# A gated pair of linear-attention blocks on one core: x's first blocks in two transfers, and the gate's weights ahead of x

## Chip, core and metric

The kernel runs on one core of a Trainium2 chip. The metric is the time of one execution in microseconds of device time; the number that counts is the median of several executions. Beside it stands the profile of one execution of its own, taken by the hardware profiler.

## What is computed

x has 2048 rows of 640 columns in bfloat16. Two attention blocks, A and B, read the same x, each with its own wqkv (640 x 1920) and wo (640 x 640). In a block there are 32 heads of 20 columns, and the attention is linear: no softmax, but a positive function phi on q and k. A gate, one number for each row of x, mixes the two outputs.

```
g = sigmoid((x * gate_w).sum(-1, keepdims=True))
a = block(x, A_wqkv, A_wo);  b = block(x, B_wqkv, B_wo)
return g * a + (1 - g) * b

block(x, wqkv, wo):
    q, k, v = heads of x @ wqkv
    pq, pk = phi(q), phi(k)              # phi(t) = (t + 1 if t > 0 else exp(t)) + 1e-6
    kv = sum over rows of pk * v;  z = sum over rows of pk
    o = (pq @ kv) / (pq . z + 1e-6)
    return o @ wo
```

## The kernel before

x lies in SBUF twice: xn has rows on the partitions, xT has columns on the partitions (five groups c of 128). k of A is computed in 16 blocks of 128 rows: for each block and each half (320 columns) five matmuls, one for each c, with xT's block as weights and wkA's part c as the moving operand (`k_mm`, line 288). Then come q, the sums over rows, and block B in the same way; the last stage forms the output rows. The order of the work is written out by hand (line 942 on), so each engine works its instructions off in the order of the program.

**The loads at the start** (lines 151 to 174). `load_x(eng, lo, hi)` loads blocks lo to hi of x's first 512 rows into xn. These rows are dealt out so that a partition holds four rows that follow each other in memory, one for each block; one block is 160 KB in pieces of 1280 bytes. `load_wk(eng, lo, hi)` loads wkA's parts lo to hi, 160 KB each. Two queues issue, SyncE (SP) and ScalarE (ACT), in this order:

- SP: block 0 of x, wkA part 0, the gate's weights g5 (1.2 KB, five partitions), wkA part 2, wkA parts 3 and 4 in one, three transfers of wqA, then 15 transposing loads (line 172) that bring the other 1536 rows of x straight into xT.
- ScalarE: block 1 of x, wkA part 1, blocks 2 and 3 of x, then the load of its table of functions.

**The first work on PE.** Seven matmuls on constants (line 206) fill the time until x arrives. `k_first` (line 311) then transposes x's blocks on PE: `x_transpose` (line 242) is five transpositions of 128 x 128 into PSUM and two copies by VectorE into xT. `gate_column` (line 217) is one more transposition, of g5, from which three small ScalarE copies (line 222) put the gate's weights beside wkA as a further column, so that the second half of each k block carries the gate's product along (321 columns). The order in `k_first` is: blocks 0 and 1 transposed, the gate column, k for blocks 0 and 1 with parts 0 and 1 of wkA (8 matmuls), block 2 transposed, part 2 for blocks 0 and 1 (4 matmuls), block 3 transposed, parts 0 to 2 for block 2 (6 matmuls), and then parts 3 and 4 for blocks 0, 1 and 2, each followed by phi on ScalarE and VectorE (`k_done`, line 295). A whole block 3 and q follow.

**Much later**, `Masks` (line 1015) runs the matmuls that are the last to read wvA and then loads wvB through `load_w` (line 859), whose last argument says where the load is cut. wvB is first read in `kv_low` (line 1056).

Of the kernel before, what the change touches and what calls it, by code (L numbers as in the profile page):

```python
# [9 lines left out]
P = 128  # L10
# [7 lines left out]
DT = D // P  # L18
ST = S // P
NB = 4  # L20
CB = 4
# [12 lines left out]
def kernel(  # L34
# [11 lines left out]
    nc = tc.nc  # L46
# [29 lines left out]
    def ps_raw(name, slot=None):  # L76

        if slot is None:
            slot = turn[0]
            turn[0] = (slot + 1) % 4  # L80
        return pools.get(slot, pools["ps"]).tile([P, 4 * HB], BF16, tag=f"ps{slot}", name=name)
# [5 lines left out]
    def ps(name, slot=None):  # L87

        return banks(ps_raw(name, slot))
# [20 lines left out]
    g5 = persist.tile([DT, P], BF16, name="g5")  # L110
# [37 lines left out]
    wv = [None, None]  # L148
    wq = [None, None]
    wk[0] = wpool.tile([P, DT, D + 2], BF16, tag="wk", name="wkA")  # L150
    def load_x(eng, lo, hi):
        eng.dma_start(out=xn[:, lo:hi, :], in_=xb0[:, lo:hi, :])

    def load_wk(eng, lo, hi):
        eng.dma_start(out=wk[0][:, lo:hi, 0:D], in_=wq_dram[0][:, lo:hi, D:2 * D])

    load_x(nc.sync, 0, 1)
    load_x(nc.scalar, 1, 2)
    load_wk(nc.sync, 0, 1)
    load_wk(nc.scalar, 1, 2)  # L160
    nc.sync.dma_start(out=g5[:], in_=gate_w.rearrange("(c p) -> c p", p=P))
    load_x(nc.scalar, 2, 3)
    load_wk(nc.sync, 2, 3)
    load_x(nc.scalar, 3, 4)
    nc.scalar.preload_act_table_set("natural_log_exp_and_others")
    load_wk(nc.sync, 3, DT)
    wq[0] = wpool.tile([P, DT, D], BF16, tag="wq", name="wqA")
# [2 lines left out]
    for n in range(1, NB):  # L170
        for c in range(DT):
            nc.sync.dma_start_transpose(
                out=xT[:, c, n * HB:(n + 1) * HB], in_=x2[n * HB:(n + 1) * HB, c * P:(c + 1) * P]
# [4 lines left out]
    for r in range(4):  # L178
# [3 lines left out]
        out=spread[:].rearrange("p (h t) -> p h t", t=TW), in_=I4[:, :, None].to_broadcast([P, H, TW])  # L182
    )
    nc.gpsimd.memset(maskE[:], 1.0)
    for lo in range(0, HF, K6):
        part = maskE[:, lo:min(lo + K6, HF)]
        for sign, base in ((1, 0), (-1, Dh - 1)):
            nc.gpsimd.affine_select(
                out=part, in_=part, pattern=[[-sign * Dh, part.shape[1] // Dh], [0, Dh]],
# [3 lines left out]
    for rows, n in ((slice(0, 2 * H), H // 2), (slice(2 * H, P), H)):  # L193
        nc.gpsimd.tensor_copy(
            out=E4_rows[rows, 0:n], in_=I4[rows, 0:n, None].to_broadcast([rows.stop - rows.start, n, Dh])
# [6 lines left out]
    warm_raw = ps_raw("warm", 0)  # L202
# [14 lines left out]
    def gate_column(pt):  # L217

        at = slice(4 * HB - 2 * P, 4 * HB - 2 * P + DT)
        nc.tensor.transpose(out=pt[:, at], in_=g5[:], identity=ident[0:DT, 0:DT])  # L220
        for lo, hi in ((0, 1), (1, 2), (2, DT)):
            nc.scalar.copy(out=wk[0][:, lo:hi, D:D + 1], in_=pt[:, at, None][:, lo:hi])
# [19 lines left out]
    def x_transpose(i, slot):  # L242
        pt = ps_raw("xt", slot)
        for c in range(DT):
            nc.tensor.transpose(out=pt[:, c * P:(c + 1) * P], in_=xn[:, i, c * P:(c + 1) * P], identity=ident[:])
        src = pt[:, 0:D].rearrange("p (c n) -> p c n", c=DT)
        for lo, hi in ((0, 2), (2, DT)):
            nc.vector.tensor_copy(out=xT[:, lo:hi, i * P:(i + 1) * P], in_=src[:, lo:hi])

    class Phi:  # L250

        def __init__(self, dst, src, lifted=False):
            self.dst, self.src, self.lifted = dst, src, lifted
            e = work.tile([P] + list(dst.shape[1:]), BF16, tag="e", name="e", bufs=4)
            self.e = e[:]
            self.parts = parts = [(self.e, dst, src)] if not isinstance(src, list) else [
                (self.e[:, n], dst[:, n], part) for n, part in enumerate(src)]
            for to, lifted_to, part in parts:
                nc.scalar.activation(out=to, in_=part, func=ACT.Exp)  # L259
                if lifted is True:  # L260
                    self.lift(lifted_to, part)
# [26 lines left out]
    def k_mm(b, i, c, pt, hf):  # L288
        n = HF + (b == 0 and hf == 1)
        nc.tensor.matmul(  # L290
            pt[:, hf, 0:n], lhsT=xT[:, c, i * P:(i + 1) * P], rhs=wk[b][:, c, hf * HF:hf * HF + n],
            start=(c == 0), stop=(c == DT - 1),
        )

    def k_done(b, i, pt, lifted=False, between=None):
        f = Phi(pk[:, i, :].rearrange("p (b n) -> p b n", b=2), pt[:, :, 0:HF], lifted)
        if b == 0:
            nc.scalar.activation(out=gl[:, i:i + 1], in_=pt[:, 1, HF:HF + 1], func=ACT.Exp)
        f.clamp()
        if between is not None:  # L300
            between()
        f.top()

    def k_chunk(b, i, slot=None, lifted=False, between=None):
        pt = ps(f"k{'AB'[b]}", slot)
        for hf in range(2):
            for c in range(DT):
                k_mm(b, i, c, pt, hf)
        k_done(b, i, pt, lifted, between)

    def k_first():

        pts = []

        def part(i, cs, hfs=(0, 1)):
            for c in cs:
                for hf in hfs:
                    k_mm(0, i, c, pts[i], hf)

        x_transpose(0, 3)  # L320
        x_transpose(1, 1)
        gate_column(warm_raw)
        pts += [ps("kA", 2), ps("kA", 3)]
        for hf in range(2):
            for i in range(2):
                part(i, (0, 1), (hf,))
        x_transpose(2, 0)
        for i in range(2):
            part(i, (2,))
        x_transpose(3, 1)  # L330
        pts.append(ps("kA", 0))
        part(2, (0, 1, 2))
        for i in range(3):
            part(i, (3, 4))
            k_done(0, i, pts[i])
        k_chunk(0, 3, 1)
# [281 lines left out]
    def kv_mm(b, banks, gs, cs=range(DT)):  # L618

        for g in gs:  # L620
            hf, n = g // 3, rows_in(g)
            part = slice(blocks[g].start - hf * HF, blocks[g].stop - hf * HF)
            for k, c in enumerate(cs):
                nc.tensor.matmul(
                    banks[hf][:n, part], lhsT=wv[b][:, c, blocks[g]], rhs=GT[hf][:, c, part],
                    start=(k == 0), stop=(k == DT - 1),
                )
# [46 lines left out]
    def cells(pt):  # L674
        return [pt[:, hf] for hf in range(2)]
# [183 lines left out]
    def load_w(b, which, eng, cuts=(0, DT)):  # L859
        lo = {"q": 0, "k": D, "v": 2 * D}[which]  # L860
        t = wpool.tile([P, DT, D], BF16, tag="w" + which, name=f"w{which}{'AB'[b]}")
        for c0, c1 in zip(cuts, cuts[1:]):
            eng.dma_start(out=t[:, c0:c1], in_=wq_dram[b][:, c0:c1, lo:lo + D])
        return t
# [76 lines left out]

    with tc.manual_schedule():
        k_first()
        turn[0] = 2
        for n in range(2):
# [8 lines left out]
        for n in range(1, NB):  # L954
            nc.sync.dma_start(
                out=xn[:, n * CB:(n + 1) * CB, :], in_=x2[n * HB:(n + 1) * HB, :].rearrange("(q p) d -> p q d", p=P)
# [58 lines left out]
        class Masks:  # L1015

            def __init__(self, slot):
                self.pt = ps("kvA", slot)
                kv_mm(0, cells(self.pt), (0, 1, 2, 3, 5, 4))
                wv[1] = load_w(1, "v", nc.sync)  # L1020

            def clamp(self):
                kv_mask(0, cells(self.pt), 0, 2)
# [97 lines left out]
        for i in range(1, half):  # L1121
            p, after = pairs[i], pairs[i + 1] if i + 1 < half else None
# [49 lines left out]
```

## Time and profile before

| | us |
|---|---|
| median of 3 executions | 183.19 (183.09 to 183.71) |
| the profiled execution, its own time | 183.32 |
| its span, first to last instruction | 181.6 |
| PE busy | 177.7 |
| VectorE busy | 148.3 |
| ScalarE busy | 107.9 |
| PE's first transposition of x | 3.83 |
| load of wkA's parts 3 and 4 issued | 3.97 |

Times inside the profile are counted from the span's start. The profile has several views: the page with each engine's busy time and the chain of work that ended last; the chain in order of time; the waits (who waited for whom); the timeline; the DMA issues with their time from issue to landing; and busy times in chosen stretches. In their lines L245 is line 245 of the kernel, PE is TensorE's matmuls, PEld its weight loads, DVE VectorE, ACT ScalarE, and SPq and ACTq are instructions with which SyncE and ScalarE issue a transfer. `xT<-xt` means that xT is written and xt read. What stands in brackets is the idle time of the engine ahead of the instruction and what ended it. A transposition is a matmul with x as weights, so it has a line under PEld and one under PE.

### The profile page before, as it was taken

Reading aid. Unit: us, or ns where it says so; the run is one execution under the profiler, and the core shown is the slowest. Engines: PE = TensorE matmul, PEld = TensorE weight load, DVE = VectorE, ACT = ScalarE, POOL = GpSimd, SP = SyncE. Lnnn points to the kernel's source line nnn. Section 1 sums busy time; section 2 is a strip of 40 time slices with the busy share of each in tenths; the row PEclk is TensorE's granted clock in tenths of the full one; section 3 lists DMA queues with packets and bytes.
Section 4 is the critical chain, followed back from the end, with each engine's and each line's share of the span. In section 5 each row is a group of like instructions: output and inputs, shape, how many; then the busy total and the mean of one; then the engine's idle time right before and its main releaser. Section 6 shows DMA issues by size and latency. Waiting matters only on the chain.

```text
span 181.6 us, 3380 instructions
## 1 busy us (share of the span) xinstructions
PE 177.7 (98%) x1284; PEld 118.5 (65%) x1284; DVE 148.3 (82%) x268; ACT 107.9 (59%) x209; POOL 5.0 (3%) x21
## 2 busy tenths in 40 slices
PE   8999999999999999999999999999999999999993
PEld 3666656655666677676666655765678777777772
DVE  0478988999999896799898987997988988686764
ACT  2066579976884512785868696964814755466210
POOL 8300000000000000000000000000000000000000
PEclk9999999999999999999999999999999999999999
DMA  5995448985102733005000000043901660322132
GB/s 172 298 178 88 93 112 251 370 173 141 48 0 58 244 120 115 0 0 180 5 0 0 0 4 0 13 146 84 291 12 31 176 159 0 110 88 96 72 131 90
DMA packets 21602, 18.85 MB, mean 104 GB/s; under 512 B 9298, under 2 KB 21074, under 8 KB 21586
## 3 DMA queue, kind: packets, MB, share of 16 engines
q1 hardware_dynamic: 20722, 17.82, 35.7%
q10 hardware_dynamic: 864, 0.82, 1.3%
q8 instruction: 10, 0.16, 0.4%
q14 instruction: 6, 0.05, 0.1%
HBM read 11.86 MB, written 4.80 MB: 92 GB/s over the span
## 4 chain that ended last, share of the span: by engine, by line
PE 93%; DMA 4%; DVE 1%; issue 0%
PE gs L510 17%; PE kB L290 12%; PE q L408 11%; PE kA L290 11%; PE qA L343 7%; PE oy L757 6%; PE oz L757 5%; PE ox L757 4%; PE ow L757 4%; PE q L343 3%; DMA wkA<-in_A_wqkv_dram 2%; PE gB L480 2%; PE gA L480 2%; DMA xn<-in_A_x_dram 2%; PE qB L343 1%; PE mA L640 1%
## 5 line engine op out<-in xcount | busy, mean ns | idle before, releaser
L290 PEld LDWEIGHTS <-xT 128*128 128x128 bf16 x320 | 30.9, 97 | 15.4 <-issue 0.4
L267 DVE TENSOR_SCALAR e<-e 128x640 bf16<-128x640 bf16 (+2 forms) x58 | 19.6, 339 | 6.1 <-ACT e L259 5.5
L290 PE MATMUL kB<-wkB,xT 128*128 128x320 bf16 x160 | 24.2, 299 | 0.0
L290 PE MATMUL kA<-wkA,xT 128*128 128x320 bf16 (+1 forms) x160 | 23.4, 299 | 0.2 <-DMA wkA<-in_A_wqkv_dram 0.2
L259 ACT ACTIVATE e<-q 128x512 bf16<-128x512 f32 x26 | 15.7, 603 | 5.2 <-PE q L408 4.1
L510 PEld LDWEIGHTS <-xn 128*128 128x128 bf16 x128 | 12.2, 98 | 6.0 <-issue 1.3
L259 ACT ACTIVATE e<-kA 128x640 bf16<-128x640 f32 x16 | 11.3, 713 | 7.8 <-PE kA L290 7.7
L259 ACT ACTIVATE e<-kB 128x640 bf16<-128x640 f32 x16 | 11.4, 710 | 7.5 <-PE kB L290 7.3
L343 PE MATMUL qA<-xT,wqA 128*128 128x512 bf16 x60 | 13.4, 379 | 0.0
L343 PEld LDWEIGHTS <-wqA 128*128 128x128 bf16 x64 | 7.5, 117 | 5.9
L278 DVE SCALAR_TENSOR_TENSOR pk<-kB,e 128x640 bf16<-128x640 f32 x12 | 9.9, 823 | 1.0
L820 ACT COPY u<-ox 128x320 f32<-128x320 f32 x8 | 3.4, 425 | 11.4 <-PE ox L757 11.4
L757 PEld LDWEIGHTS <-xT 128*128 128x128 bf16 x85 | 8.1, 98 | 2.9
L757 PEld LDWEIGHTS <-pqTA 128*128 128x128 bf16 x85 | 8.0, 98 | 2.8
L762 DVE TENSOR_TENSOR osb<-oz,u 128x320 bf16<-128x320 f32 (+2 forms) x18 | 8.0, 453 | 2.2 <-PE oz L757 1.8
L757 PEld LDWEIGHTS <-pqTB 128*128 128x128 bf16 x80 | 7.8, 98 | 3.0
L510 PE MATMUL gs<-pk,xn 128*128 128x320 bf16 x64 | 9.4, 299 | 0.0
L278 DVE SCALAR_TENSOR_TENSOR pk<-kA,e 128x640 bf16<-128x640 f32 x10 | 8.2, 823 | 0.9
L426 DVE TENSOR_TENSOR q<-q,p 128x512 f32<-128x512 f32 x12 | 8.3, 692 | 0.8 <-PE q L408 0.6
L259 ACT ACTIVATE e<-qA 128x1024 bf16<-128x1024 f32 x6 | 6.2, 1027 | 4.2 <-PE qA L343 3.9
L480 PEld LDWEIGHTS <-xn 128*128 128x128 bf16 x64 | 6.3, 98 | 3.0
L510 PEld LDWEIGHTS <-S 128*128 128x128 bf16 x64 | 6.0, 98 | 2.5 <-issue 0.3
(183 smaller groups left out, 348.1 us busy)
## 6 DMA issues: line engine op xcount, KB each, us to landing
out_dram<-osb SPq DMA_DIRECT2D x14, 160.0 KB, 1.8
xn<-in_A_x_dram SPq DMA_DIRECT2D x3, 640.0 KB, 6.7
wvA<-in_A_wqkv_dram SPq DMA_DIRECT2D x1, 800.0 KB, 12.0
wkB<-in_B_wqkv_dram SPq DMA_DIRECT2D x1, 800.0 KB, 4.5
wqB<-in_B_wqkv_dram SPq DMA_DIRECT2D x1, 800.0 KB, 5.3
wvB<-in_B_wqkv_dram SPq DMA_DIRECT2D x1, 800.0 KB
MA<-m_rows SPq DMA_DIRECT2D x1, 800.0 KB, 5.3
MB<-m_rows SPq DMA_DIRECT2D x2, 400.0 KB, 4.3
```

What stands on the lines that cost most here:

```text
L259: nc.scalar.activation(out=to, in_=part, func=ACT.Exp)
L267: nc.vector.tensor_scalar(self.e, self.e, 1.0, EPS, op0=ALU.min, op1=ALU.add)
L278: nc.vector.scalar_tensor_tensor(out=dst, in0=src, scalar=1.0 + EPS, in1=e, op0=ALU.add, op1=ALU.max)
L290: nc.tensor.matmul(pt[:, hf, 0:n], lhsT=xT[:, c, i * P:(i + 1) * P], rhs=wk[b][:, c, hf * HF:hf * HF + n], start=(c == 0), stop=(c == DT - 1),
L343: nc.tensor.matmul(dst, lhsT=mixed(wq[b][:, c, :], m), rhs=xT[:, c, n * HB:(n + 1) * HB], start=first, stop=last,)
L408: nc.tensor.matmul(dst, lhsT=left(c), rhs=right(c), start=first and k == 0, stop=k == len(cs) - 1, skip_group_check=not first,)
L426: nc.vector.tensor_tensor(out=dst, in0=src, in1=sb, op=ALU.add)
L480: nc.tensor.matmul(pt[:, hf, 0:HF], lhsT=xn[:, i, c * P:(c + 1) * P], rhs=pk[:, i, hf * HF:(hf + 1) * HF], start=(i == 0), stop=(i == ST - 1),
L510: nc.tensor.matmul(pt[:, n, 0:HF], lhsT=left[:, i, n * P:(n + 1) * P], rhs=right[:, i, :], start=(first and i == 0), stop=(i == hc - 1), s ...
L757: nc.tensor.matmul(dst, lhsT=left[:, c, r0:r0 + P], rhs=right[:, c, :], start=(first and c == 0), stop=(c == DT - 1), skip_group_check=not ...
L762: nc.vector.tensor_tensor(out=dst, in0=acc, in1=sb, op=ALU.add)
L820: nc.scalar.copy(out=self.u2[:], in_=self.at("x"))
```

## The change

At the start, x's first four blocks come as two transfers of two blocks each, the first on SP and the second on ScalarE; since a partition's two blocks lie side by side in memory, a piece is now 2560 bytes. g5 moves from SP's third place to ScalarE's first. wkA's part 0 moves from SP to ScalarE, part 1 from ScalarE to SP. In `k_first` the gate column stands in front of the transpositions. wvB is loaded in three transfers instead of one.

```diff
-    load_x(nc.sync, 0, 1)
-    load_x(nc.scalar, 1, 2)
-    load_wk(nc.sync, 0, 1)
-    load_wk(nc.scalar, 1, 2)
-    nc.sync.dma_start(out=g5[:], in_=gate_w.rearrange("(c p) -> c p", p=P))
-    load_x(nc.scalar, 2, 3)
+    load_x(nc.sync, 0, 2)
+    nc.scalar.dma_start(out=g5[:], in_=gate_w.rearrange("(c p) -> c p", p=P))
+    load_wk(nc.scalar, 0, 1)
+    load_wk(nc.sync, 1, 2)
+    load_x(nc.scalar, 2, CB)
     load_wk(nc.sync, 2, 3)
-    load_x(nc.scalar, 3, 4)
     nc.scalar.preload_act_table_set("natural_log_exp_and_others")
     load_wk(nc.sync, 3, DT)
...
+        gate_column(warm_raw)
         x_transpose(0, 3)
         x_transpose(1, 1)
-        gate_column(warm_raw)
         pts += [ps("kA", 2), ps("kA", 3)]
...
-                wv[1] = load_w(1, "v", nc.sync)
+                wv[1] = load_w(1, "v", nc.sync, (0, 2, 4, DT))
```

## The prediction

> **What bounds the kernel now.** I read the page first, for the share of each engine and the chain that ended last.
>
> ```profile
> PE 177.7 (98%) x1284; PEld 118.5 (65%) x1284; DVE 148.3 (82%) x268; ACT 107.9 (59%) x209; POOL 5.0 (3%) x21
> PE 93%; DMA 4%; DVE 1%; issue 0%
> ```
>
> PE is the bound, and the only other thing with a share worth naming is 4% of waiting for DMA. The chain of waits in order of time, cut to the first 36 us, says where that is (start, length, what); the last line is a later piece of the same view, kept for its price.
>
> ```profile
> 0.81 3.15 DMA xn<-in_A_x_dram
> 3.96 0.02 issue
> 3.97 4.47 DMA wkA<-in_A_wqkv_dram
> 8.44 0.04 issue
> 8.49 3.17 PE kA L290 x22
> ...
> 70.60 2.72 PE kB L290 x20
> ```
>
> The reader is to see two transfers, one released by the other: a block of x lands at 3.96, only then is a part of wkA issued, and PE goes on at 8.49 when that part is there. Twenty matmuls of 320 columns take 2.72 us, so one costs 0.136 us. Next the busy times in stretches (columns: stretch, its length, PE, PEld, DVE, ACT, POOL busy, granted clock, DMA share, GB/s).
>
> ```profile
> 3.00:5.40 2.40, 2.34 (x17) 1.24 (x15) 0.81 (x4) 1.29 (x4) 2.27 (x8) 1.00 1.03 359
> 5.40:6.40 1.00, 1.00 (x11) 0.77 (x11) 0.20 (x1) 0.00 (x0) 0.57 (x2) 1.00 0.76 184
> ...
> 8.50:181.60 173.10, 170.30 (x1238) 114.29 (x1237) 146.01 (x257) 106.33 (x205) 0.00 (x0) 1.00 0.36 98
> ```
>
> After 8.50 PE is busy 170.30 of 173.10 us: what moves the start of that dense stretch moves the end by as much, and nothing in the stretch can give it back. Before it, the DMA engines carry 359 GB/s, and drop to 184 between 5.4 and 6.4: a hole in the loads, in front of the very load that PE waits for. The DMA queues' waits and PE's wait explain the hole.
>
> ```profile
> SPq L155 <- DMA xn<-in_A_x_dram: 1.5, 1, 1.5
> ```
>
> ```profile
> PE kA L290 <- DMA wkA<-in_A_wqkv_dram: 0.2, 1, 0.2
> ```
>
> SP stands 1.5 us at line 155, which loads weights, until a block of x has landed; no tile joins the two. The issues in order of time (start, length, queue) show why.
>
> ```profile
> 0.81 0.39 SPq L152 DMA_DIRECT2D xn<-in_A_x_dram  x1
> 1.26 0.42 SPq L155 DMA_DIRECT2D wkA<-in_A_wqkv_dram  x1
> 1.73 0.36 SPq L161 DMA_DIRECT2D g<-in_gate_w_dram  x1
> 2.13 2.23 SPq L155 DMA_DIRECT2D wkA<-in_A_wqkv_dram  x2
> 4.41 1.49 SPq L169 DMA_DIRECT2D wqA<-in_A_wqkv_dram  x3
> ```
>
> ```profile
> 1.25 0.46 ACTq L155 DMA_DIRECT2D wkA<-in_A_wqkv_dram  x1
> 1.74 0.94 ACTq L152 DMA_DIRECT2D xn<-in_A_x_dram  x2
> ```
>
> By 2.7 us eight transfers are issued: SP's two blocks of weights, x and g, and on ScalarE these three behind one of x at 0.81. The ninth is wkA's last part, and it waits for one of the first two. I read this as eight completion counters used in turn; that reading is an inference, and it is a rival below that it is wrong.
>
> **The path to 8.49.** These rows are PE's and its weight loads', in order of time.
>
> ```profile
> 3.83 0.94 PEld L245 LDWEIGHTS <-xn 128*128 128x128 bf16 x10 [0.75 <-DMA xn<-in_A_x_dram]
> 4.88 0.17 PE L220 MATMUL warm<-ident,g 5*128 5x5 bf16 x1
> 4.99 0.85 PE L290 MATMUL kA<-wkA,xT 128*128 128x320 bf16 x4
> 5.39 0.11 PEld L290 LDWEIGHTS <-xT 128*128 128x128 bf16 x2 [0.29 <-DVE xT L248]
> 6.09 0.40 PEld L245 LDWEIGHTS <-xn 128*128 128x128 bf16 x5
> 8.02 0.30 PE L290 MATMUL kA<-wkA,xT 128*128 128x321 bf16 x1
> ```
>
> The last matmul ahead of the stall starts at 8.02, so the next was due at 8.02 + 0.136 = 8.16 and starts at 8.49: the stall is worth 0.33 us (the 0.2 in the view of the waits counts the modelled tail of a matmul as busy). From the first transposition, at 3.83, to the due time are 4.33 us, in which PE waits only for VectorE's copies (0.29 at 5.39).
>
> **The change part by part.** First the times to landing of the transfers (the last column, us from issue).
>
> ```profile
> xn<-in_A_x_dram SPq DMA_DIRECT2D x1, 160.0 KB, 3.0
> xn<-in_A_x_dram ACTq DMA_DIRECT2D x1, 160.0 KB, 3.2
> wkA<-in_A_wqkv_dram ACTq DMA_DIRECT2D x1, 160.0 KB, 3.5
> xn<-in_A_x_dram ACTq DMA_DIRECT2D x1, 160.0 KB, 4.1
> wkA<-in_A_wqkv_dram SPq DMA_DIRECT2D x1, 320.0 KB, 4.5
> wqA<-in_A_wqkv_dram SPq DMA_DIRECT2D x1, 320.0 KB, 5.5
> ```
>
> *The stall goes.* Seven transfers now stand ahead of wqA, so none up to wkA's last part is a ninth. That part is SP's fourth issue, at about 2.13, as the third weight part was; with its own 4.5 us it lands at 6.6, with the slowest row, 5.5 us, at 7.6. PE wants it at 8.16 or later: hidden by 0.5 us at least. Gain 0.33 us. The ninth transfer is now wqA's second part, which waits for x's first landing, about 4.0, and is issued at 4.0 instead of 4.91 (4.41 and a third of 1.49); the 15 transposing loads behind it start some 0.8 us earlier too. PE never waits for either in the dense stretch, so that brings nothing.
>
> *The first two blocks come as one transfer.* PE's first transposition now needs 320 KB, not 160. From below: 3.0 us, as block 0 alone. From above: 4.5 us, the row of a 320 KB transfer. I take 3.2 us: by that time both blocks are in SBUF today, over the two queues, with the same weight parts beside them, and the same bytes pass through the same DMA engines. So x lands at 0.81 + 3.2 = 4.01, PE starts 0.02 later, as it does now, at 4.03 instead of 3.83, and reaches the due time at 4.03 + 4.33 = 8.36. Loss 0.20 us.
>
> The Trainium skill ("DMA: Bandwidth & Descriptors", "Anatomy of one DMA") fits a transfer as 2.0 us and its bytes at 436 GB/s, for GpSimd's path; by that, 160 KB more cost an estimated 0.38 us, and the due time would be 8.54, with no gain left. Block 0's row of 3.0 us is above the 2.4 that the fit gives for it, so it doesn't hold here as it stands.
>
> *What comes behind it.* Needs are today's starts and 0.20. wkA's second part, SP's second issue at 1.26, is wanted by the second k matmul (4.99 + 0.136 + 0.20 = 5.33), and until 5.45 a delay is hidden, because the third matmul waits for VectorE's copy until 5.59 anyway: with 3.5 us it lands at 4.8, with 4.1 at 5.4, with 4.5 at 5.8, which would cost 0.3. I take nothing. Blocks 2 and 3, at 1.74 on ScalarE, are wanted at 6.29 and land at 5.8 (4.1 us) or 6.2 (4.5 us): hidden. ScalarE issues three transfers instead of four, so its table load moves forward; nothing on it is wanted before the gate column.
>
> *The gate product moves ahead.* Its 0.17 us at 4.88 leave the place between the transpositions and the first k matmul, and fall before x arrives. There the gain is at least 0 and at most the 0.10 us to the next issue; I take 0, since the VectorE copy at 5.39 sets the third k matmul. Now every transposition stands behind it on PE. Its 1.2 KB are ScalarE's first issue, at 0.81: taken as slow as the 160 KB that stand there today, they land at 4.01, with x. No loss. The three gate copies on ScalarE follow earlier.
>
> *wvB in three parts.* The queue's rows and the first use:
>
> ```profile
> 81.67 0.38 SPq L863 DMA_DIRECT2D wvB<-in_B_wqkv_dram  x1
> 116.94 1.49 SPq L649 DMA_DIRECT2D m_rows<-MA  x3
> ```
>
> ```profile
> 136.53 0.74 PE kvB L624 x15
> ```
>
> Two more issues of about 0.4 us fall where SP is free for 34 us, 50 us ahead of the use: nothing.
>
> **The sum.** -0.33 + 0.20 = -0.13 us. The profiled execution took 183.32 us, 1.7 above its span of 181.6, and would take 183.19; the median shown is 183.19, 0.13 below the profiled one, so the forecast against it is 183.06.
>
> **The rivals.** (a) *The doubled transfer eats the whole gain:* block 1's 164,000 bytes come behind block 0's, at the 359 GB/s of the stretch from 3.00 to 5.40, which is 0.46 us; x lands at 4.27, PE starts at 4.29 and is due at 8.62, and the time is 183.32, no change. The point where gain turns to loss is a landing at 3.81 + 0.33 = 4.14, and the forecast is only 0.13 away from it. For it: one queue instead of two carries the bytes.
> (b) *The change does not free SP:* if the ninth transfer's wait is for x's data and not for a counter, wkA's last part is issued after 4.01 and lands 4.5 later, at 8.51: 183.23, again no change. Against it: wqA's issue at 4.41 follows without a wait.
> (c) *Slower, through the first transfer:* 320 KB in one transfer took 4.5 us where it was measured. Then PE starts at 5.33, is due at 9.66, and everything is 1.17 us late: 184.36. Against it: that transfer started on an emptied queue, and its bytes came in 256 pieces, where x's two blocks lie side by side.
> (d) *Slower, through PE's rate.* These rows are weight loads between warm-up matmuls of 512 columns, and ten later matmuls of that width:
>
> ```profile
> 1.65 0.15 PEld L206 LDWEIGHTS <-const-bfloat16-1.0 128*128 128x128 bf16 x1 [0.28 <-issue]
> 2.08 0.15 PEld L206 LDWEIGHTS <-const-bfloat16-1.0 128*128 128x128 bf16 x1 [0.28 <-issue]
> ```
>
> ```profile
> 108.28 2.16 PE qB L343 x10
> ```
>
> They come 0.43 us apart at first and 0.216 later: PE starts at half rate, though the clock column shows 1.00. 128 columns are then 0.107 us and later 0.054. The weight loads of the first ten transpositions span 0.94 us, one of them 0.10, so their step is 0.84/9 = 0.093: the rate rises while they run. If the longer gap before them, some 0.15 us more, puts that off, the work of 5.2 to 8.4 runs at half rate for up to 3.2 us and ends up to 1.6 us later; with half of that, 183.06 + 0.8 = 183.86. The Trainium skill ("TensorE: Matmul & The Clock Gate", "Part 4: PE-mode transpose") says that transpositions do not count as activity for the clock, which would give this rival. The rate rising among transpositions speaks against it here.
>
> **How the numbers follow.** Forecast 0.56, (a) 0.14, (b) 0.06, (c) 0.12, (d) 0.08, and 0.04 for a gain beyond all of these. Within 0.3% (0.55 us), about what a measurement of this kernel can tell from no change, lie the forecast, (a) and (b): 0.76. Slower are (c) and (d): 0.20. Faster by more has 0.04, since the rows allow at most 0.33 + 0.10 = 0.43 us. The lower end is that bound, 182.76; the upper end takes in (a), (b) and the cheaper half of (d), up to 183.85.
>
> **What would show it.** Right: SP's wait at line 155 for x is gone; wkA's last part lands before 7.7; the first transposition starts at 4.0 to 4.1; PE has no wait for wkA, and the dense stretch starts at about 8.36. Wrong: a first transposition after 4.16, a wait of kA for wkA's second part near 5.3, or k matmuls at 0.27 us after 5 us. The whole fails if PE finds new waits after 8.5.

## The result, and the profile after

The changed kernel takes 184.31 us (median of 10 runs, 182.88 to 184.97), the kernel before beside it 183.19 (10 runs, 182.84 to 183.71): a ratio over the runs of 1.0048 with a 95% interval of 1.0028 to 1.0069 (the quotient of the two medians is 1.0061). It is slower, by about half a per cent, where the forecast was 183.06 and no change. The profiled execution took 184.02 us with a span of 182.3, 0.70 us more than that of before.

The page's busy times and its shares of the chain that ended last, of the kernel after:

```profile
PE 177.5 (97%) x1284; PEld 118.2 (65%) x1284; DVE 148.2 (81%) x268; ACT 107.9 (59%) x209; POOL 5.0 (3%) x21
PE 94%; DMA 3%; DVE 1%; ACTq 1%; issue 0%
```

No engine has more work than before, and the share of DMA in the chain even fell from 4% to 3%. A share says nothing on when that wait stands, so the chain in order of time comes next (start, length, what).

```profile
1.80 5.40 DMA xn<-in_A_x_dram
7.20 0.05 issue
7.25 0.45 PE xt L243 x5
...
8.53 3.84 PE kA L288 x28
```

The wait for wkA's last part is gone from it. In its place stands x's second pair, blocks 2 and 3: issued at 1.80, landed at 7.20, and PE's next transposition right behind it. The timeline of PE, before and after, prices the two (start, length, instructions; the bracket is the idle time ahead and what ended it). Before:

```profile
6.22 0.44 PE L245 MATMUL xt<-ident,xn 128*128 128x128 bf16 x5
11.49 1.24 PE L343 MATMUL qA<-xT,wqA 128*128 128x512 bf16 x5
```

After:

```profile
3.71 0.18 PE L218 MATMUL warm<-ident,g 5*128 5x5 bf16 x1
3.86 0.84 PE L243 MATMUL xt<-ident,xn 128*128 128x128 bf16 x10
4.90 1.37 PE L288 MATMUL kA<-wkA,xT 128*128 128x320 bf16 x8 [0.19 <-DMA wkA<-in_A_wqkv_dram]
7.25 0.45 PE L243 MATMUL xt<-ident,xn 128*128 128x128 bf16 x5 [0.98 <-DMA xn<-in_A_x_dram]
12.20 4.05 PE L341 MATMUL qA<-xT,wqA 128*128 128x512 bf16 x18
```

Block 2 is transposed at 7.25 instead of 6.22, 1.03 us later. From there to q's first matmul PE takes 4.95 us instead of 5.27: these 0.32 are the old stall for wkA, which the forecast had priced at 0.33. What is left is 12.20 - 11.49 = 0.71 us, and that is the whole difference, as the stretches from q's first matmul to the end show (columns as in the prediction). Before and after:

```profile
11.49:181.60 170.11, 167.31 (x1218) 112.15 (x1215) 144.63 (x255) 104.24 (x199) 0.00 (x0) 1.00 0.34 96
```

```profile
3.00:5.40 2.40, 2.21 (x17) 1.15 (x16) 0.94 (x4) 0.86 (x4) 2.27 (x8) 1.00 1.02 345
5.40:6.40 1.00, 0.86 (x6) 0.39 (x4) 0.08 (x1) 0.00 (x0) 0.57 (x2) 1.00 0.78 227
6.40:7.20 0.80, 0.00 (x0) 0.00 (x0) 0.00 (x0) 0.00 (x0) 0.00 (x0) 1.00 0.94 290
...
12.20:182.30 170.10, 167.31 (x1218) 112.17 (x1215) 144.60 (x255) 104.25 (x199) 0.00 (x0) 1.00 0.33 94
```

170.11 us against 170.10, with the same 167.31 of PE. The first row carries the surprise: between 3.00 and 5.40 the DMA engines were full before (a share of 1.03) and are full after (1.02). They move no more in that time; they move something else. The timeline of SP and the DMA issues with their time to landing (the last column, in us) say what:

```profile
0.81 0.40 SPq L152 DMA_DIRECT2D xn<-in_A_x_dram  x1
1.27 1.37 SPq L155 DMA_DIRECT2D wkA<-in_A_wqkv_dram  x3
2.68 1.55 SPq L167 DMA_DIRECT2D wqA<-in_A_wqkv_dram  x3
```

```profile
xn<-in_A_x_dram ACTq DMA_DIRECT2D x1, 320.0 KB, 5.4
wkA<-in_A_wqkv_dram SPq DMA_DIRECT2D x1, 320.0 KB, 6.3
```

SP no longer waits ahead of wkA's last part. That part, 320 KB, is issued at about 2.2 instead of 3.97, and wqA's first two parts, 320 KB each, at 2.68 and 3.20 instead of from 4.41 on. So 960 KB of weights are out by 3.3 us, while x's second pair is under way. The pair takes 5.4 us, where blocks 2 and 3 took 4.1 each. And the weights gain nothing: issued at 2.2 with 6.3 us to landing, wkA's last part is there at 8.5, as before (3.97 + 4.47 = 8.44).

So the theory after the result, called **crowding** below: SP's wait in the kernel before did harm at its own place, 0.33 us, but it also kept these weights off the DMA engines for 1.8 us in which x was under way, and x was wanted sooner. Its rivals are the **size** (two blocks in one transfer are slow to land), the **gate** in front (PE's clock or ScalarE's queue) and **wvB's three parts**. The expectations below call crowding "backlog", and they name one rival more, **order**: transfers are served in the order of issue, so that weights issued behind x could not slow it.

### The profile page after: what moved, and what is told of

Its sections match the earlier page's. It is cut to its first block, busy times and chain, and to the rows that moved or that the text cites. A ratio compares the mean times of both kernels' runs of the same rounds, so it can differ in the third digit from the quotient of the medians.

```text
span 182.3 us, 3381 instructions
## 1 busy us (share of the span) xinstructions
PE 177.5 (97%) x1284; PEld 118.2 (65%) x1284; DVE 148.2 (81%) x268; ACT 107.9 (59%) x209; POOL 5.0 (3%) x21
## 4 chain that ended last, share of the span: by engine, by line
PE 94%; DMA 3%; DVE 1%; ACTq 1%; issue 0%
PE gs L508 17%; PE kB L288 12%; PE q L406 11%; PE kA L288 11%; PE qA L341 7%; PE oy L755 6%; PE oz L755 5%; PE ox L755 4%; PE ow L755 4%; DMA xn<-in_A_x_dram 3%; PE q L341 3%; PE gB L478 2%; PE gA L478 2%; PE qB L341 1%; PE mA L638 1%; PE kvA L622 1%
```

## The experiments

Each kernel ran beside the kernel before on the same chip; ratios are to that one. "After" and "before" ahead of a diff name the kernel that it changes.

**a1: after once more**, without an edit.

> The changed kernel as it stands, a second profile of it, for the spread. All theories: about 184.3 us against 183.2 before. If x's second pair is late by its place and size, its landing is again near 7.2 and PE's wait for block 2 near 1 us; if the lateness is chance, landing and time move together from run to run (182.9 to 185.0 have been seen).

184.58 us (6 runs), ratio 1.0069 [1.0048, 1.0089]. The second pair landed 6.0 us after its issue, at 7.81, and q began at 12.81. The profile shown above was a good one of its kind.

**a2: the second pair as two transfers** (after).

```diff
-    load_x(nc.scalar, 2, CB)
+    load_x(nc.scalar, 2, 3)
     load_wk(nc.sync, 2, 3)
+    load_x(nc.scalar, 3, CB)
```

> Blocks 2 and 3 in two transfers again, all else as changed; eight transfers up to wkA's last part, so SP still doesn't wait. Theory 'size' (PE waits for 320 KB where 160 would do): block 2 lands 0.5 to 1 us earlier, near 6.2 to 6.7, time 183.4 to 183.8. Theory 'backlog' (weights issued early crowd x out): block 2 lands as late as the pair did, near 7, time 184.3. Theory 'order' (served in the order of issue): block 2 earlier by 0.4, but block 3, now issued beside wkA's last part, lands after 7; time 183.6 to 184.2.

184.62 us (6 runs), 1.0063 [1.0042, 1.0083], the same as a1. Block 2 landed at 6.80 and block 3 at 7.84. Block 2 alone, 160 KB, took 4.99 us, where before it took 4.1. The size of the transfer isn't the cause. Order isn't excluded by these landings (block 2 earlier than the pair at 7.20, block 3 later); c1 and d1 decide on it.

**a3: the last part earlier still** (after). wkA's part 2 goes to ScalarE, behind the pair, so that SP issues the last part, and wqA behind it, one place earlier.

```diff
-    load_wk(nc.sync, 2, 3)
+    load_wk(nc.scalar, 2, 3)
```

> wkA's part 2 goes to ScalarE's queue behind x's second pair, all else as changed. Theory 'order': the pair comes 164,000 bytes earlier, 0.4 us, near 6.8, and the time falls by 0.4 to 183.9. Theory 'backlog': wkA's last part moves up to about 1.75 on SP, so the pair is crowded as much or more: time 184.3 or above. Theory 'size': no change, 184.3.

185.88 us (6 runs), 1.0146 [1.0110, 1.0182], twice a1's loss. The view of the waits (us in total, times, longest) has PE's weight loads and its transpositions standing for x:

```profile
PEld L243 <- DMA xn<-in_A_x_dram: 2.6, 1, 2.6
PE xt L243 <- DMA xn<-in_A_x_dram: 2.2, 1, 2.2
```

The pair landed at 8.39, and wkA's part 2, now the last on ScalarE, at 9.34. PE stands for that part too:

```profile
9.38 0.71 PE L288 MATMUL kA<-wkA,xT 128*128 128x320 bf16 x4 [0.49 <-DMA wkA<-in_A_wqkv_dram]
```

These matmuls start 0.94 us behind block 2's first transposition (8.44), where in the kernel after it is 0.29, so some 0.65 us of this loss belong to the place of part 2. Only the rest, x landing later than in any profile of the kernel after, speaks for crowding.

**a4: an attempt to hold SP** (after), with two further loads of the gate's weights into tiles that nobody reads, so that the transfers behind them come later in the turn of the counters.

```diff
+    for _ in range(2):
+        spare_g = persist.tile([DT, P], BF16, name=f"spare{_}")
+        nc.scalar.dma_start(out=spare_g[:], in_=gate_w.rearrange("(c p) -> c p", p=P))
     nc.scalar.preload_act_table_set("natural_log_exp_and_others")
```

> Two more transfers of 1.2 KB (the gate's weights into tiles that nothing reads) stand ahead of wkA's last part, which is then the ninth and waits, as in the kernel before, until the first transfer has landed, about 3.9; all else as changed. This also tests the reading of eight counters: SP should show a wait of about 1 us again. Theory 'backlog': with the weights held back x's second pair lands near 5.9 to 6.2, PE's wait for it falls below 0.2 us, time 183.2 to 183.5. Theories 'order' and 'size': the pair is issued ahead of the held part in any case and lands as late as now; time 184.3.

185.06 us (6 runs), 1.0118 [1.0076, 1.0160]. It did not hold what it should: the built program issues wkA's last part at 2.19, and only wqA waits until 3.8. The pair landed at 8.12. With the last part alone, 320 KB instead of 960, the loss is no smaller than a1's, so the amount of weights isn't what decides. (What else its profile shows is told at the end.)

**b1: holding the last part alone** (after). VectorE writes one column of wkA's part 3 from x's first pair, so that part can be loaded only behind that pair's landing.

```diff
+    nc.vector.tensor_copy(out=wk[0][:, 3, 0:1], in_=xn[:, 0, 0:1])
     load_wk(nc.sync, 3, DT)
```

> The changed kernel, with wkA's last part held on SP until x's first pair has landed: VectorE writes one column of that part from x's first block, and the load, which overwrites it, has to wait for that write (the two small transfers of the earlier attempt held only wqA back). The issue should come near 3.9 instead of 2.2. Theory 'backlog' (the early weights crowd x out): x's second pair lands near 5.9 to 6.4, PE's wait for it falls from 1.1 to 1.6 us to 0.3 or less, time 183.2 to 183.7. Theories 'order' and 'size': the pair as late as now, 7.2 to 7.8, time 184.3 to 184.6.

184.84 us (6 runs), 1.0085 [1.0056, 1.0114]. The last part was issued at 3.87, but the built program put one part of wqA, 320 KB too, at 2.20 in its place. In the profiled execution, the fastest of the six (183.63), the pair landed at 6.81 and PE stood 0.35 us for it. That is a4 the other way round, with the same outcome in the median: whichever weights take the place at 2.20, x is late. Neither a4 nor b1 kept both away.

**b2: the wait gone, and little else** (before). g5 is issued by GpSimd, which leaves seven transfers on the other two queues ahead of the last part.

```diff
-    nc.sync.dma_start(out=g5[:], in_=gate_w.rearrange("(c p) -> c p", p=P))
+    nc.gpsimd.dma_start(out=g5[:], in_=gate_w.rearrange("(c p) -> c p", p=P))
```

> The kernel before with one edit: the gate's weights are issued from GpSimd, so that wkA's last part is no longer the ninth transfer and SP doesn't wait; everything else of the change is left out. Theory 'backlog': the removed wait is by itself harmful: wkA's last part is issued near 2.2, blocks 2 and 3 land 0.5 to 1.5 us later than 5.85 and 6.3, PE waits for them, time 183.7 to 184.5. The prediction on record: the wait is pure loss, time 182.9 to 183.1. If GpSimd's transfer still counts among the eight, the wait stays and the time is 183.2.

183.81 us (12 runs), 1.0041 [1.0026, 1.0056]: x in four transfers, the gate where it was, wvB in one, and yet most of the loss. SP's timeline and the issues with their time to landing:

```profile
0.82 0.40 SPq L152 DMA_DIRECT2D xn<-in_A_x_dram  x1
1.27 1.37 SPq L155 DMA_DIRECT2D wkA<-in_A_wqkv_dram  x3
3.72 1.40 SPq L169 DMA_DIRECT2D wqA<-in_A_wqkv_dram  x3
```

```profile
xn<-in_A_x_dram ACTq DMA_DIRECT2D x3, 160.0 KB, 5.1
wkA<-in_A_wqkv_dram SPq DMA_DIRECT2D x1, 320.0 KB, 5.8
```

The wait in front of wkA's last part is gone, and the wait now stands in front of wqA. So the wait goes by the count of transfers and not by x's data: the counters' turn is shown. x's blocks on ScalarE take 5.1 us in the median instead of 4.1. In this profile PE ran at half rate until about 6.2, so it was due at block 2 only at 6.65 (its last k matmul started at 6.51 and takes 0.14); it began at 6.91, behind the landing at 6.86. An earlier full rate would not have moved that start, which the landing sets. Against the kernel before, block 2 is 0.69 us later (6.91 after 6.22), the stall of 0.33 us is gone, and q begins 0.45 us later, at 11.94. The other path of g5 costs nothing here: k begins at 4.93 after 4.99.

**b3: x ahead of the weights** (after). SP issues the second pair as two blocks, ScalarE wkA's part 2.

```diff
-    load_x(nc.scalar, 2, CB)
-    load_wk(nc.sync, 2, 3)
+    load_x(nc.sync, 2, 3)
+    load_wk(nc.scalar, 2, 3)
+    load_x(nc.sync, 3, CB)
```

> The changed kernel with the loads in the order in which PE needs them: on SP x's first pair, wkA's part 1, x's block 2, x's block 3, wkA's last part; on ScalarE the gate's weights, wkA's parts 0 and 2. Theory 'backlog': behind x in the same queue the last part can't crowd it; block 2 lands before 6, block 3 near 6.3, PE's waits for x are below 0.2 us and what is left is the wait for the last part, near 8.4; time 183.0 to 183.4. Theory 'chance of slow DMA engines': blocks 2 and 3 still late, 184 or more.

183.31 us (12 runs), 1.0013 [1.0000, 1.0026]. Block 2 landed at 6.11 and block 3 at 6.91; the last part, issued at 2.67, at 7.99. q began at 11.50, as before. Putting the weights behind x on SP's own queue takes most of the loss back. The 0.33 us are not won; in this profile PE was at half rate until 5.9 and came to block 2 at 6.56, so it doesn't say whether they could be.

**b4: the gate part undone** (after): g5 third on SP, the gate column behind the transpositions.

```diff
-    nc.scalar.dma_start(out=g5[:], in_=gate_w.rearrange("(c p) -> c p", p=P))
     load_wk(nc.scalar, 0, 1)
     load_wk(nc.sync, 1, 2)
+    nc.sync.dma_start(out=g5[:], in_=gate_w.rearrange("(c p) -> c p", p=P))
...
-        gate_column(warm_raw)
         x_transpose(0, 3)
         x_transpose(1, 1)
+        gate_column(warm_raw)
```

> The changed kernel with the gate part undone: the gate's weights third on SP, their product behind the transpositions. x's second pair is now ScalarE's second transfer, issued near 1.25 instead of 1.8 and ahead of wkA's parts 1 and 2. Theory 'backlog': the pair lands about 0.5 to 1 us earlier, near 6.3, wkA's part 1 may be late instead, time 183.3 to 184.0. If the gate's place itself costs time, it shows as a kA wait or start that the landing doesn't explain; I expect none.

185.32 us (6 runs), 1.0101 [1.0071, 1.0131]: worse, not better. Without g5 ahead of it the second pair moves up to 1.23 on ScalarE and lands at 5.54, but PE's first transposition then starts at 4.45 instead of 3.86, wkA's part 1 lands at 5.79, and PE's first k matmul starts at 6.12 instead of 4.90. What it waits for last is the gate itself, whose 1.2 KB took 4.2 us:

```profile
6.02 0.17 PE L218 MATMUL warm<-ident,g 5*128 5x5 bf16 x1 [0.84 <-DMA g<-in_gate_w_dram]
```

So with these loads the gate is late in its old place, and its move to the front is no cause of the loss. The edit moved the crowd to other transfers, so it doesn't price the gate alone. Nor does this profile show the whole of the median: it is one of the two fast executions (183.79 and 183.98), and the other four took 185.30 to 185.51.

**c1: holding everything** (after), with three loads into unread tiles, on SP itself and ahead of the last part.

```diff
+    for n in range(3):
+        spare = persist.tile([DT, P], BF16, name=f"spare{n}")
+        nc.sync.dma_start(out=spare[:], in_=gate_w.rearrange("(c p) -> c p", p=P))
     load_wk(nc.sync, 3, DT)
```

> The changed kernel with three transfers of 1.2 KB (the gate's weights into tiles that nothing reads) on SP ahead of wkA's last part, which becomes the tenth and waits for x's first pair; wqA stays behind it in the queue, so that nothing takes the held place (in the earlier attempt a part of wqA was issued at 2.2 instead). SP's wait of the kernel before is back, near 3.9; all else is as changed. Theory 'backlog': x's second pair lands near 5.9 to 6.3, PE's wait for it is below 0.3 us at full rate, time 183.2 to 183.7. If the pair's double size or its place is the cause, it lands near 7 as before and the time is 184.3.

184.34 us (12 runs), 1.0051 [1.0034, 1.0068]. The head of the profile did what it should: last part issued at 3.93, the pair landed at 6.69, q begun at 11.70 instead of 12.20. But the rest took 171.40 us instead of 170.10, with a wait of PE for a transfer that no other profile here has:

```profile
151.32 0.97 PE L758 MATMUL ow<-MB,pqTB 128*128 128x320 bf16 x6 [0.55 <-DMA MB<-m_rows]
```

Three more transfers shift the turn of every later one. That this made the late waits is only argued; d1 was built to keep the count.

**c2: the order of need in the kernel before** (before, with g5 on GpSimd as in b2).

```diff
-    nc.sync.dma_start(out=g5[:], in_=gate_w.rearrange("(c p) -> c p", p=P))
-    load_x(nc.scalar, 2, 3)
-    load_wk(nc.sync, 2, 3)
-    load_x(nc.scalar, 3, 4)
+    nc.gpsimd.dma_start(out=g5[:], in_=gate_w.rearrange("(c p) -> c p", p=P))
+    load_x(nc.sync, 2, 3)
+    load_wk(nc.scalar, 2, 3)
+    load_x(nc.sync, 3, 4)
```

> The kernel before, with the gate's weights issued from GpSimd (so SP doesn't wait) and the loads in the order of need: on SP x's block 0, wkA's part 0, x's blocks 2 and 3, wkA's last part; on ScalarE x's block 1, wkA's parts 1 and 2. Theory 'backlog': without SP's wait, and with x ahead of the last part in one queue, blocks 2 and 3 land near 5.7 and 6.5, the last part near 8.0 instead of 8.44; the stall of 0.33 us goes and nothing takes its place: 182.8 to 183.1, and 0.6 to 1 us below the kernel that only drops the wait (183.81). If the loads aren't what decides, 183.8.

183.76 us (12 runs), 1.0013 [0.9996, 1.0030]. Beside b2, the same direction as b3 beside after: with x's blocks first on SP, block 2 lands at 6.14 instead of 6.86, and the ratio falls from 1.0041 to 1.0013. By the medians less comes back, 0.66 to 0.43 us above the kernel before, and the 182.8 to 183.1 hoped for were missed. One cost is the edit's own: g5, from GpSimd, landed at 5.03 here, and k began at 5.18 instead of 4.99.

**d1: everything held, and the count kept** (c1, with wqA in two transfers instead of three and wvB in one, so that from there on as many transfers stand ahead of each later one as in the kernel before).

```diff
-    for lo, hi in ((0, 2), (2, 4), (4, DT)):
+    for lo, hi in ((0, 2), (2, DT)):
         nc.sync.dma_start(out=wq[0][:, lo:hi, :], in_=wq_dram[0][:, lo:hi, 0:D])
...
-                wv[1] = load_w(1, "v", nc.sync, (0, 2, 4, DT))
+                wv[1] = load_w(1, "v", nc.sync)
```

> As c1 (wkA's last part held on SP until x's first pair has landed), but with wvB in one transfer and wqA in two, so that as many transfers come ahead of every later one as in the kernel before, and each completion counter is used at the same places. c1 had PE stalls of 0.30 us at 16.9 and 0.72 at 151.3 in its profile that no other run had; with equal counts they should go. Theory 'backlog': x's second pair lands near 6.0 to 6.7, and the time is 183.1 to 183.6. If holding the weights back doesn't help, 184.3.

183.47 us (11 runs), 1.0003 [0.9992, 1.0014]. The paired x, the gate in front and the other order on ScalarE are all still there; SP's wait is back, and the loss is gone. (What wqA's cut does by itself is open; but c1, with wqA in three, had its pair and q early too. wvB's cut is d2.) SP's timeline, the issues with their time to landing, and PE's timeline:

```profile
2.20 1.01 SPq L166 DMA_DIRECT2D spare<-in_gate_w_dram  x3
3.71 0.42 SPq L155 DMA_DIRECT2D wkA<-in_A_wqkv_dram  x1
4.56 0.99 SPq L170 DMA_DIRECT2D wqA<-in_A_wqkv_dram  x2
```

```profile
xn<-in_A_x_dram ACTq DMA_DIRECT2D x1, 320.0 KB, 4.1
wkA<-in_A_wqkv_dram SPq DMA_DIRECT2D x1, 320.0 KB, 3.2
```

```profile
6.29 0.44 PE L246 MATMUL xt<-ident,xn 128*128 128x128 bf16 x5
...
11.23 2.11 PE L344 MATMUL qA<-xT,wqA 128*128 128x512 bf16 x8
```

The pair took 4.1 us, not 5.4, and the last part 3.2, not 6.3: issued 1.5 us later than in the kernel after, it landed 1.6 us earlier, at 6.9. In this profile PE waits for neither, and q begins 0.26 us before it does in the kernel before. This also answers order: the pair is issued at 1.80 as in the kernel after, ahead of the held part in both, and still lands earlier.

**d2: wvB in one transfer** (after, the last hunk alone undone).

> The changed kernel with only the wvB part undone (one transfer again). The prediction's step says that part is worth nothing: 184.3 to 184.6, as the changed kernel. If it serves to give the later transfers the same counters as before, undoing it brings late stalls and costs up to 1 us more: 185.

184.66 us (6 runs), 1.0089 [1.0056, 1.0122]. With a1's 1.0069 that is no difference: wvB's parts are worth nothing either way.

**d3: the old stall by another way** (before). wkA's last part comes as two loads, wqA as two, and PE takes part 3 for blocks 0 and 1 ahead of part 4, so that the first half is enough to go on with.

```diff
-    load_wk(nc.sync, 3, DT)
+    load_wk(nc.sync, 3, 4)
+    load_wk(nc.sync, 4, DT)
...
+        for i in range(2):
+            part(i, (3,))
         for i in range(3):
-            part(i, (3, 4))
+            part(i, (4,) if i < 2 else (3, 4))
```

> The kernel before, its wait on SP kept, with wkA's last part loaded as two (and wqA in two transfers, for equal counts), and PE taking part 3 for blocks 0 and 1 ahead of part 4. If what is left to win is the 0.33 us stall on the last part, and x isn't to be crowded, this wins it: part 3 lands before 8.2, part 4 is wanted 0.5 us later; time 182.8 to 183.0 against 183.2. If the parts come no earlier, or phi's chain of block 0, which starts 0.27 us later, makes q wait, no change: 183.2.

183.47 us (12 runs), 1.0002 [0.9988, 1.0016]. The halves landed at 7.37 and 7.82, and the stall is gone from the profile without any crowding; yet the median stands still. The chain in order of time shows what fills the place:

```profile
0.85 2.93 PE warm L207 x7
3.78 1.21 PE xt L246 x10
4.99 0.12 PE warm L221
5.11 2.00 PE kA L291 x8
```

It is PE without a gap, but eight k matmuls take 2.00 us, 0.25 each and not 0.136: PE was at half rate until 6.9 in this execution, and q began at 11.98. In the kernel before a late full rate is partly absorbed by the stall, which here it isn't. That this is why the 0.33 us are not seen in the median is an argument from single profiles, not shown: no run sets the moment of the full rate.

**e1, e2, e3: the three kernels again**, before, d1 and after, for a further profile of each.

> The kernel before, a second profile, for the spread. Blocks 2 and 3 land by 6.5 and PE doesn't wait for them; the first full-rate matmul comes anywhere between 4 and 6.6 us, and the wait for wkA's last part is smaller by as much as the half rate has cost by then. If the half rate always ends near 4.7 here and later in the other kernels, it is the change that moves it.

> d1 again, a second profile: x's second pair lands by 6.5, PE has no wait of more than 0.4 us for it. A landing near 7 would say that d1's profile was luck and that the held weights aren't what decides.

> The changed kernel, a third profile: x's second pair lands between 6.7 and 8, as in the two profiles so far (7.2 and 7.8), and q's first matmul starts 0.5 us or more after the 11.5 of the kernel before.

Before 183.33 us (8 runs, 1.0009 [0.9985, 1.0033]), d1 183.56 (8 runs, 1.0003 [0.9989, 1.0017]), after 184.65 (4 runs, 1.0067 [1.0027, 1.0107]). By profile:

| | x's later blocks landed | q's first matmul | the execution, us |
|---|---|---|---|
| before | 5.82 and 6.28 | 11.49 | 183.32 |
| before (e1) | 5.61 and 6.20 | 11.62 | 183.55 |
| d1 | 5.94 | 11.23 | 183.06 |
| d1 again (e2) | 6.72 | 11.72 | 183.65 |
| after | 7.20 | 12.20 | 184.02 |
| after (a1) | 7.81 | 12.81 | 184.62 |
| after (e3) | 7.55 | 12.55 | 184.37 |
| d2, the same loads at the start as after | 6.92 | 11.92 | 183.92 |

The landing scatters by up to 0.9 us from execution to execution with the same loads, so single profiles overlap nearly: d2's 6.92 is only 0.2 above e2's 6.72. But in this table the four with the loads of after lie above all the others, among the three of after the time follows the landing one to one (0.61 us of landing, 0.60 of time), and the medians part clearly: 183.47 and 183.56 with the weights held, 184.31 to 184.66 without. e2 also missed what was hoped of it, a landing by 6.5: with the pair at 6.72, PE waited for x for some 0.7 us. The hold trades the old stall for a wait that comes and goes, and so it equals the kernel before and does not beat it. No version tried here does.

## Why the prediction was wrong

**The step that failed** is the one that put blocks 2 and 3 "at 5.8 (4.1 us) or 6.2 (4.5 us): hidden". The 4.1 comes from a trace in which SP stood still for 1.5 us and sent no further weights beside x; the edit that ends this wait takes that away. (The 4.5 is of the transfer behind the wait.) The pair took 5.4, 6.0 and 5.7 us in three profiles of the kernel after, and 5.1 in d2's. The margin was 0.1 to 0.5 us, so an addition of a microsecond is a loss at once: 1.03 us in the profile shown. The forecast put this term at nothing; with it the sum of that profile is -0.32 + 1.03 = 0.71 us instead of -0.13.

**"The stall goes"**: right in what it says of PE and of SP. The counters' turn was read rightly (b2, d1), the wait is gone, and PE's path lost 0.32 of the 0.33 us. But the last part did not land "at 6.6, with the slowest row, 5.5 us, at 7.6"; it landed at 8.5. The stall vanished only since PE came later itself. The drop to 184 GB/s between 5.4 and 6.4 was read as a hole that an earlier issue would fill: it is still there at 227 GB/s, and its DMA share is 0.78 after 0.76. And of the ninth transfer and what follows it the prediction asked what they bring, "nothing", not what they take from others. That transfer, wqA's second part, didn't wait until 4.0 either: the completion counter on which it waits in the trace is g5's, and it went out at 3.20.

**"The first two blocks come as one transfer"**, loss 0.20 us: too high. The first transposition started at 3.86 instead of 3.83, so the pair had landed at most 3.05 us after its issue (2.9 to 3.1 in the six profiles of other variants that record it). Rivals (a) and (c), which rest on a later landing, fall with it; that (c)'s 184.36 lies near the 184.31 measured is chance.

**The gate product, wkA's second part, wvB**: the gate stands at 3.71, ahead of x, and costs nothing; d1, which keeps it in front, equals the kernel before. wkA's second part landed at 4.66, ahead of its use at 5.03, as forecast. What k waits for at 4.90, by 0.19 us, is the first part, which now stands second on ScalarE (issued at 1.40, landed at 4.85); the prediction didn't price it, and it moves no start: k begins at 4.90 after 4.99 before. wvB is nothing by d2.

**"Nothing in the stretch can give it back"**: right: 170.10 us from q's first matmul, to 0.01 of before.

**Rival (d)**, half rate: not the cause here. The eight k matmuls took 1.37 us in the profile of after, and full rate came at about 4.1 against 4.7 before. In d2's profile half rate did last, until about 6.6, and yet q began there at 11.92, the earliest of the four with these loads: PE had to stand for x anyway.

The rival that came true, that the wait shielded x, was not among the four. Rival (b) asked whether SP is freed, none asked whom a freed SP hurts, and the wait for x's second pair was not among the signs of being wrong. The Trainium skill ("DMA: Bandwidth & Descriptors", "Issuing engines are not separate DMA queues") says that transfers from all issuing engines run on the same 16 DMA engines and interleave. The trace agrees: ScalarE's x was slowed from 4.1 to 5.1 us in b2 by what SP issued. The Trainium skill, on the same page ("Rules for kernel authors"), advises issuing a transfer early and waiting for it late, to overlap it with work; in d1 the transfer issued 1.5 us later landed 1.6 us earlier, and in e2 one issued 1.6 us later landed 1.0 us earlier, so here the measurement decides.

## What to carry to other kernels

A wait on an issuing queue is also a gate: before counting it as loss, list every transfer behind it with its bytes, and ask which transfer that is wanted sooner shares the DMA engines with them at that time. Where the engines were already full (a share of 1.02 to 1.03 here), issuing earlier moved no more bytes in that time; it changed who was late. So issue in the order of need. And a landing time read from a trace holds only for that crowd: where the margin is a few tenths, price the step with the crowd that the change makes.

## What the runs showed of the hardware beside that

PE's full rate comes at very different times: by the spacing of its instructions, between 4.0 and 6.9 us in 18 profiles (4.7 and 4.5 in the two of the kernel before, 4.1, 4.6 and 5.6 in the three of after), while the clock column reads 1.00 over the stretch from 3.00 to 5.40 in the kernels before and after. The Trainium skill ("TensorE: Matmul & The Clock Gate", "What's actually happening") has the rate rise with a window that runs freely, so that the moment varies by 0.5 us to either side; here it varied by 0.75 us to either side in the three profiles of after, and by 1.45 us over all the variants, nearly three times the 0.5.

In one profile the rate was lost again behind a gap. In a4 PE was idle for 1.8 us before block 2; that stretch and the two that follow (columns as before):

```profile
6.40:8.20 1.80, 0.03 (x1) 0.04 (x2) 0.00 (x0) 0.00 (x0) 0.00 (x0) 0.96 0.97 343
8.20:11.50 3.30, 3.30 (x19) 2.36 (x20) 1.11 (x4) 0.00 (x0) 0.00 (x0) 0.50 0.83 170
11.50:15.00 3.50, 3.50 (x27) 2.45 (x26) 1.54 (x4) 2.19 (x7) 0.00 (x0) 1.00 0.39 88
```

The granted clock is 0.50 for 3.3 us, which puts q's first matmul at 14.70 and that execution at 186.72 us. In a3's profile a wait for x of 2.2 us had no such end, so a gap is not enough by itself. What decides it stayed open, as did the late waits of c1.
